# A weight conversion spread over six slots, and output products two tiles behind the gate in the first token block

## The chip, the cores and the metric

One core of one Trainium2 chip. TensorE multiplies matrices, VectorE and ScalarE work on elements, GpSimd does a few small operations, SyncE (SP) issues nearly all DMAs. The metric is device time in microseconds (us), the median of several executions.

## What is computed

Block attention, a gated feed-forward layer with RMS norm, and a second feed-forward layer with a rational activation, over 4608 tokens of width 512, all in float32:

```python
def _attn_ref(q, k, v):            # (8, 8, 576, 64), in chunks of 64 tokens
    scores = scale * np.matmul(q_c, k_c.transpose(0, 1, 2, 4, 3))
    scores = scores - np.max(scores, axis=-1, keepdims=True)
    attn = np.exp(scores)
    attn = attn / (np.sum(attn, axis=-1, keepdims=True) + 1e-09)
    return np.matmul(attn, v_c)

def _moe_ref(x, w_gate, w_val, w_out, rms_g):      # 512 -> 1536 -> 512
    rms = np.sqrt(np.mean(x * x, axis=-1, keepdims=True) + 1e-06)
    xn = x / rms * rms_g
    g = xn @ w_gate
    silu = g * (1.0 / (1.0 + np.exp(-g)))
    return silu * (xn @ w_val) @ w_out

def _moe2_ref(x, w_in, w_out, a, b):               # 512 -> 2048 -> 512
    h = x @ w_in
    P = a[0] + a[1] * h + a[2] * h**2 + a[3] * h**3
    Q = 1.0 + np.abs(b[0]) * np.abs(h) + np.abs(b[1]) * h**2
    return (P / (Q + 1e-06)) @ w_out
```

The weights of both layers reach the device as raw 64-bit words, two 32-bit words each, and the kernel turns each into a pair of rounded float32 numbers, a high and a low part.

## The kernel before

The tokens are cut into nine blocks j of 512, the 1536 features of the first layer into twelve tiles f of 128, those of the second into sixteen. Phase 1 runs over j and f, phase 2 over j and its sixteen tiles. Every matrix product is three passes (high x high, high x low, low x high) over four slices of depth: 12 matmuls of 128x512.

A **unit** u holds the three weight matrices of feature tile f=u: gate, val and output. It is converted once, in block 0, by six operations that `words_to_pair` lists after one DMA: L110 (ScalarE, first scaling), L114 (ScalarE, low word into `t`), L116 (VectorE, shift), L118 (VectorE, add), L121 (ScalarE, cast to the high part), L123 (VectorE, low part). Units 0 and 1 are converted in thirds, unit 2 and 3 as wholes; all of that and the first three feature tiles are interleaved by hand: each letter of `START` steps one generator (0 to 4 are attention tiles, a to f thirds of units 0 and 1, g, h, i are units 2, 3, 4, M, N, P the feature tiles 0, 1, 2, and each O is one output product). Units 4 to 11 are converted in the loop behind `START`.

That loop has three **slots** per feature tile: slot 3f holds the gate (12 matmuls, then tanh L386 on ScalarE and L388 on VectorE), slot 3f+1 val (12 matmuls, then L396 on VectorE, the cast L399 on ScalarE, L401 on VectorE, which give the pair r), slot 3f+2 one output product `p1_gemm2` (12 matmuls) of an earlier tile from the list `pend`. Ahead of a slot's own work `slot()` emits what the attention plan has there; behind it `weights(j, at)` emits the steps of units that `at_slots` put there, in the order in which they were entered, which is rising u. In block 0 the attention of block 1 has a tile each six slots: products (`xs`, with L250, L227, L229 on VectorE and L259, L236 on ScalarE) ahead of the gate of f=3, 5, 7, 9, a scale L356 two slots later, and transposes (`tp`, with L285, L292, L241 and the reciprocal on VectorE, L282 and L290 on ScalarE) ahead of val of f=4, 6, 8, 10.

The schedule is manual: each engine's instructions stand in the order in which the code emits them, and the waits are derived from the data and from the reuse of buffers. Buffers come from pools: 13 of "s3" (start tiles, raw words, converted units, later the stages of the second layer's weights), 3 of "s4" (the pairs r), 8 of "s2" (attention temporaries and u), 2 PSUM tiles "mm" for gate and val in turn, one "at" for attention, two "acc" for the output products.

Of the kernel before, what the change touches and what calls it, by code (L numbers as in the profile page):

```python
# [12 lines left out]
U32 = mybir.dt.uint32  # L13
# [6 lines left out]
P = 128  # L20
W = 512
CH = 64
U = 3
# [1 line left out]

START = (
    "0120d31230af041b0e0c1g002001012d21d02dd3011021d310320130123013230a3212a31321432aa13424a213a432bM"
    "3bb2b432e3bdcMbccecMMe4ecMMecgh4N4egMgNMgfNMgNONfghfPfhhNhfPNhfiOPhPPPP"
)

@with_exitstack
def fused_kernel(
# [36 lines left out]
    NSTART = 3  # L69
# [6 lines left out]
    def s3(name, shape=(P, U, 2, W), dtype=F32R):  # L76
        return sb.tile(list(shape), dtype, tag="s3", bufs=NS3, name=name)
# [22 lines left out]

    wt = {}

    def words_to_pair(high, low, t, hi, lo):

        nc.scalar.activation(  # L110
            out=high.bitcast(F32), in_=high.bitcast(F32), func=AF.Prelu, scale=2.0 ** -112, alpha=2.0 ** 32
        )
        yield
        nc.scalar.mul(t.bitcast(I32), low, 2.0 ** -29)  # L114
        yield
        nc.vector.tensor_scalar(out=high, in0=high, scalar1=3, scalar2=None, op0=ALU.logical_shift_left)  # L116
        yield
        nc.vector.tensor_tensor(out=high, in0=high, in1=t, op=ALU.add)  # L118
        yield
        x = high.bitcast(F32)  # L120
        nc.scalar.copy(hi, x)  # L121
        yield
        nc.vector.tensor_tensor(out=lo, in0=x, in1=hi.bitcast(F32), op=ALU.subtract)  # L123
        yield

    buffers = {}

    def unit(u, keys, part=None):

        if u not in buffers:  # L130
            buffers[u] = s3(f"raw{u}", (P, U, W, 2), U32), s3(f"w{u}", (P, 2, U, W))
        raw, whole = buffers[u]
        p = slice(0, U) if part is None else slice(part, part + 1)
        nc.sync.dma_start(
            out=raw[:, p].rearrange("p t f two -> p t (f two)"),
            in_=w1[u * U:u * U + U][p].rearrange("t p f -> p t f"),
        )
        yield
        for t, key in list(enumerate(keys))[p]:
            wt[key] = whole[:, :, t]  # L140
        if part is None:
            t = sb.tile([P, U, W], U32, tag="t", bufs=1, name=f"t{u}")
        else:
            t = att[(u * U + part) % TB].at[:, 5:6].bitcast(U32)
        yield from words_to_pair(raw[:, p, :, 1], raw[:, p, :, 0], t, whole[:, 0, p, :], whole[:, 1, p, :])

    w2d = [dram.tile([P, 2, U, W], F32, tag=f"w2d_{u}", name=f"w2d_{u}") for u in range(-(-2 * NF2 // U))]

    def stage(t):

        buf = s3(f"stage{t}")
        raw = buf[:, 0].rearrange("p two f -> p (two f)").bitcast(U32)
        pair = buf[:, 1]
        nc.sync.dma_start(out=raw, in_=w2[t])
        yield
        raw = raw.rearrange("p (f two) -> p f two", two=2)
        low = buf[:, 2, 0].bitcast(U32)
        yield from words_to_pair(raw[:, :, 1], raw[:, :, 0], low, pair[:, 0, :], pair[:, 1, :])
        nc.sync.dma_start(out=w2d[t // U][:, :, t % U], in_=pair.bitcast(F32))
        yield  # L160

    def unit2(u, keys):
        whole = s3(f"w2_{u}", (P, 2, U, W))
        n = len(keys)
        nc.sync.dma_start(out=whole[:, :, :n].bitcast(F32), in_=w2d[u][:, :, :n])
        for t, key in enumerate(keys):
            wt[key] = whole[:, :, t]
        yield
# [152 lines left out]
    def begin(i):  # L321

        start = i < TB
        yield from load(i, start)
        t = att[i]
        yield from products(None, t)
        yield from transposes(None, t)
        if start:
            yield from products(t, None)
            yield from transposes(t, None)  # L330

    def attention_plan(j):

        plan = {}
        if j + 1 == NB:
            return plan
        first = (j + 1) * TB

        starts = []
        gap, at, behind = (6, 9, 4) if j == 0 else (9, 1, 3)  # L340
        for n in range(TB):
            nxt = first + n + 1
            starts.append((at + n * gap, first + n, nxt if nxt < NB * TB else None))
        for at, x, s in starts:
            if s is not None:
                plan.setdefault(max(at - 3, 3 * NSTART if j == 0 else 0), []).append((loads, s))
            plan.setdefault(at, []).append((both, products, x, s))
            plan.setdefault(at + behind - 2, []).append((scale, x))
            plan.setdefault(at + behind, []).append((both, transposes, x, s))
        return plan  # L350
# [27 lines left out]
    pend = []  # L378
# [31 lines left out]
    def p1_products():  # L410
        while True:
            p1_gemm2()
            yield
# [43 lines left out]
    with tc.manual_schedule():  # L457

        def split(keys):
            return [keys[n:n + U] for n in range(0, len(keys), U)]  # L460

        first = split([(n, f) for f in range(NF1) for n in "gvo"])
        second = [unit2(u, keys) for u, keys in enumerate(split([(n, f) for f in range(NF2) for n in "iq"]))]
        work = {}

        def at_slots(x, slots, steps):
            for at, n in zip(slots, steps):
                work.setdefault(divmod(at, 3 * NF1), []).append((x, n))

        units = [None, None] + [unit(u, keys) for u, keys in enumerate(first)][2:]  # L470
        for u in range(4, NF1):
            slots = (3 * u - 10, 3 * u - 6, 3 * u - 5, 3 * u - 4, 3 * u - 3)
            at_slots(units[u], [max(at, 3 * NSTART) for at in slots][u == 4:], (1, 1, 2, 2, 1)[u == 4:])
        span = (NB - 2) * 3 * NF1
        for t in range(2 * NF2):
            at = 3 * NF1 + t * span // (2 * NF2)
            at_slots(stage(t), (at, at + 2, at + 3, at + 4, at + 5), (1, 2, 2, 2, 1))
        for u, x in enumerate(second):
            at_slots(x, ((NB - 1) * 3 * NF1 + 3 * u,), (1,))

        def weights(j, at):
            for x, n in work.pop((j, at), ()):
                for _ in range(n):
                    next(x)

        att.update((i, Tile(i, True)) for i in range(TB))
        gens = {str(i): begin(i) for i in range(TB + 1)}
        gens |= dict(zip("abcdef", (unit(u, first[u], t) for u in range(2) for t in range(U))))
        gens |= dict(zip("ghi", units[2:]))
        half = ((0, W // 2), (W // 2, W))  # L490
        gens |= dict(zip("MNP", (p1_cell(0, f, ((0, W),) if f else half) for f in range(NSTART))))
        gens["O"] = p1_products()
        next(gens["0"])
        nc.scalar.preload_act_table_set("exp_and_others")
        make_identity(nc, ident)
        nc.vector.memset(mhalf, -0.5)
        nc.vector.memset(lnb, (1.0 + 1e-6) * TWO_M63)
        nc.vector.memset(expb, -LN63)
        for step in START[START.index("0") + 1:]:
            next(gens[step])  # L500
            if step == "3" and "loaded" not in gens:
                gens["loaded"] = nc.sync.dma_start(out=gcol, in_=rms_g.rearrange("(k p) -> p k", p=P))
        nc.sync.dma_start(out=ab[:, 0:4], in_=pa.rearrange("(o n) -> o n", o=1).to_broadcast([P, 4]))
        nc.sync.dma_start(out=ab[:, 4:6], in_=pb.rearrange("(o n) -> o n", o=1).to_broadcast([P, 2]))
        nc.scalar.activation(out=absb1, in_=b1, func=AF.Abs)


        for j in range(NB):
            plan = attention_plan(j)
            at = 0 if j else 3 * NSTART  # L510

            def slot():
                for what, *of in plan.get(at, ()):
                    what(*of)

            def behind():
                nonlocal at
                weights(j, at)
                at += 1

            for f in range(0 if j else NSTART, NF1):
                if j == NB - 1 and f in (2, 3, 4, 5):
                    load_x2(0, f - 2)
                if j == NB - 1 and f in (3, 4, 5, 6):
                    split_x2(0, f - 3)
                slot()
                *_, u = p1_gate(j, f)
                behind()
                slot()
                run(p1_val(j, f, u))  # L530
                behind()
                slot()
                if len(pend) > 1:
                    p1_gemm2()
                behind()


    with tc.manual_schedule(engines={mybir.EngineType.Activation, mybir.EngineType.DVE}):
# [65 lines left out]
        for s in range(NS + 3):  # L604
            if s < NS:
                j, f = steps[s]
# [83 lines left out]
```

## Time and profile before

| | |
|---|---|
| median of 3 runs | 1794.75 us (1794.58 to 1794.98) |
| profiled execution | 1796.3 us |
| its span in the trace | 1794.5 us |
| mean granted TensorE clock | 0.996 of full speed |
| TensorE busy | 1761.6 us, 98% |

All times in a trace are counted from the span's start. "Busy" is the time in which an engine executes; matmuls are pipelined, so a busy TensorE isn't one at its peak. The page gives the whole span by engine, a table of stretches gives it by time, and the timeline gives single instructions.

### The profile page before, as it was taken

What the parts mean: (1) busy time and instruction counts of PE and PEld (TensorE: products, weight loads), DVE (VectorE), ACT (ScalarE), POOL (GpSimd) and SP (SyncE); (2) the same over time, 40 slices, a digit from 0 to 9 for tenths busy, and PEclk for the clock granted to TensorE, in tenths of its full rate; (3) what the DMA queues carried; (4) which work ended last, traced back from release to release, by engine and by line L of the source; (5) the groups of instructions that cost most, each with busy time, mean ns of one, the idle gap of its engine ahead of it and who ended that gap; (6) DMA issues with size and microseconds to landing.
All of it is one profiled execution on the core that took longest, in us unless ns stands there. A gap on an engine that the chain in (4) does not pass through costs nothing.

```text
span 1794.5 us, 24867 instructions
## 1 busy us (share of the span) xinstructions
PE 1761.6 (98%) x9960; PEld 1449.2 (81%) x9960; DVE 1144.9 (64%) x1693; ACT 913.7 (51%) x1485; POOL 261.8 (15%) x258
## 2 busy tenths in 40 slices
PE   6889999999999999999999999999999999999998
PEld 5668888888788888888888888888888888888887
DVE  8675444454444544544422688888888888888886
ACT  7563333332333333332221577777777677767775
POOL 0000000000000000000000132322233232323222
PEclk9999999999999999999999999999999999999999
DMA  9322213132222322212155201010101010101000
GB/s 355 138 89 83 94 54 107 53 107 83 100 72 83 104 68 95 88 65 94 43 193 189 88 13 41 7 41 7 41 7 41 7 48 1 48 0 48 0 24 24
DMA packets 51492, 127.44 MB, mean 71 GB/s; under 512 B 5680, under 2 KB 5680, under 8 KB 50096
## 3 DMA queue, kind: packets, MB, share of 16 engines
q1 hardware_dynamic: 51232, 125.59, 20.2%
q8 instruction: 78, 1.28, 0.3%
q14 instruction: 38, 0.31, 0.1%
q10 hardware_dynamic: 144, 0.26, 0.0%
HBM read 90.18 MB, written 35.65 MB: 70 GB/s over the span
## 4 chain that ended last, share of the span: by engine, by line
PE 91%; DVE 5%; issue 2%; ACT 1%; DMA 0%; POOL 0%; SPq 0%; DVEq 0%; ACTq 0%; POOLq 0%
PE o L585 22%; PE h L370 21%; PE vl L370 15%; PE a L427 15%; PE g L370 15%; PE xs L212 2%; DVE raw L118 1%; PE tp L275 1%; DVE w L123 1%; PE tp L278 1%; DVE raw L116 0%; DVE u L396 0%; DVE r L401 0%; DVE u L388 0%; DVE mx L227 0%
## 5 line engine op out<-in xcount | busy, mean ns | idle before, releaser
L585 PE MATMUL o<-w,gg 128*128 128x512 f32 x1728 | 416.4, 390 | 0.5 <-POOL gg L575 0.5
L370 PE MATMUL h<-x,w 128*128 128x512 f32 x1728 | 414.9, 389 | 0.0
L585 PEld LDWEIGHTS o<-w,gg 128*128 128x128 f32 x1728 | 323.6, 188 | 70.6 <-DVE ob L599 2.3
L370 PEld LDWEIGHTS h<-x,w 128*128 128x128 f32 x1728 | 324.3, 188 | 67.4
L370 PE MATMUL g<-xT,w 128*128 128x512 f32 (+1 forms) x1308 | 319.0, 393 | 11.5 <-DVE u L388 3.9
L370 PE MATMUL vl<-xT,w 128*128 128x512 f32 (+1 forms) x1308 | 320.2, 394 | 0.0
L427 PE MATMUL a<-r,w 128*128 128x512 f32 x1296 | 312.2, 389 | 1.8 <-DVE r L401 1.7
L370 PEld LDWEIGHTS g<-xT,w 128*128 128x128 f32 x1308 | 245.9, 190 | 66.1 <-DVE w L123 5.9
L427 PEld LDWEIGHTS a<-r,w 128*128 128x128 f32 x1296 | 243.1, 188 | 53.4 <-DVE r L401 2.5
L370 PEld LDWEIGHTS vl<-xT,w 128*128 128x128 f32 x1308 | 240.5, 189 | 49.3 <-DVE u L396 0.2
L575 POOL TENSOR_TENSOR gg<-T,gg 128x512 fp32r<-128x512 f32 x144 | 187.1, 1300 | 565.1 <-ACT gg L574 474.2
L388 DVE SCALAR_TENSOR_TENSOR u<-u,g 128x512 f32<-128x512 f32 x108 | 74.3, 688 | 302.5 <-ACT u L386 302.5
L386 ACT ACTIVATE u<-g 128x512 f32<-128x512 f32 x108 | 64.5, 597 | 290.3 <-PE g L370 290.2
L554 ACT ACTIVATE V<-h 128x512 f32<-128x512 f32 x144 | 86.0, 598 | 181.6 <-PE h L370 181.4
L399 ACT CAST r<-u 128x512 fp32r<-128x512 f32 x108 | 67.0, 621 | 214.0 <-DVE u L396 214.0
L557 DVE SCALAR_TENSOR_TENSOR V<-V,small,R 128x512 f32<-128x512 f32 x144 | 108.4, 753 | 78.3 <-ACT R L555 78.3
L261 POOL TENSOR_SCALAR ssq<-ssq 128x1 f32<-128x1 f32 x36 | 7.3, 203 | 852.1 <-ACT xf L259 833.8
L567 DVE SCALAR_TENSOR_TENSOR V<-V,R 128x512 f32<-128x512 f32 x144 | 99.9, 694 | 44.8 <-ACT R L566 44.8
L568 DVE SCALAR_TENSOR_TENSOR V<-V,R 128x512 f32<-128x512 f32 x144 | 124.1, 862 | 4.9
L401 DVE TENSOR_TENSOR r<-u,r 128x512 fp32r<-128x512 f32 x108 | 74.8, 693 | 73.4 <-ACT r L399 73.4
L396 DVE TENSOR_TENSOR u<-u,vl 128x512 f32<-128x512 f32 x108 | 72.6, 672 | 71.7 <-PE vl L370 71.7
L556 ACT ACTIVATE T<-h,small 128x512 f32<-128x512 f32 x144 | 112.6, 782 | 0.0
(107 smaller groups left out, 1535.0 us busy)
## 6 DMA issues: line engine op xcount, KB each, us to landing
stage<-in_w_dram SPq DMA_DIRECT2D x32, 512.0 KB, 3.7
w2d<-stage SPq DMA_DIRECT2D x32, 512.0 KB, 3.0
raw<-in_w_dram SPq DMA_DIRECT2D x10, 1536.0 KB, 8.8
w<-w2d SPq DMA_DIRECT2D x10, 1536.0 KB, 6.5
x2d<-x SPq DMA_DIRECT2D x36, 256.0 KB, 2.4
x2r<-x2d SPq DMA_DIRECT2D x36, 256.0 KB, 3.2
out_dram<-ob SPq DMA_DIRECT2D x36, 256.0 KB, 2.2
q<-in_qkv_dram SPq DMA_DIRECT2D x32, 256.0 KB, 3.7
```

The lines of the kernel that those rows point to most:

```text
L370: nc.tensor.matmul(out=acc[:, ts], lhsT=w[:, wh, wk], rhs=x[:, kk, xh, ts], start=kk == 0 and n == 0, stop=kk == KD - 1 and n == 2,)
L388: nc.vector.scalar_tensor_tensor(out=u, in0=u, scalar=1.0, in1=g, op0=ALU.add, op1=ALU.mult)
L396: nc.vector.tensor_tensor(out=u, in0=u, in1=vl, op=ALU.mult)
L401: nc.vector.tensor_tensor(out=r[:, 1, :], in0=u, in1=r[:, 0, :].bitcast(F32), op=ALU.subtract)
L427: nc.tensor.matmul(out=acc1[j][m], lhsT=wt["o", f][:, wh, ms], rhs=r[:, xh, :], start=f == 0 and n == 0, stop=f == NF1 - 1 and n == 2,)
L554: nc.scalar.activation(out=V, in_=h, func=AF.Square)
L556: nc.scalar.activation(out=T, in_=h, func=AF.Identity, scale=a3, bias=a2)
L557: nc.vector.scalar_tensor_tensor(out=V, in0=V, scalar=absb1, in1=R, op0=ALU.mult, op1=ALU.add)
L567: nc.vector.scalar_tensor_tensor(out=V, in0=V, scalar=1.0 + 1e-6, in1=R, op0=ALU.add, op1=ALU.mult)
L568: nc.vector.scalar_tensor_tensor(out=V, in0=V, scalar=-2.0, in1=R, op0=ALU.add, op1=ALU.mult)
L575: nc.gpsimd.tensor_tensor(out=r[:, 1, :], in0=T, in1=r[:, 0, :].bitcast(F32), op=ALU.subtract)
L585: nc.tensor.matmul(out=acc2[j][m], lhsT=r[:, rh, ms], rhs=wt["q", f][:, wh, :], start=f == 0 and n == 0, stop=f == NF2 - 1 and n == 2,)
```

## The change

- `unit` takes the buffer of the converted unit when the cast L121 is emitted and no longer together with the raw words' buffer at the load.
- The seven steps of a unit stand in six slots and not five: load, L110, L114 and L116, L118, L121, L123 in slots 3u-10, 3u-7, 3u-6, 3u-5, 3u-4, 3u-3. Before it was load, L110, L114 and L116, L118 and L121, L123 in 3u-10, 3u-6, 3u-5, 3u-4, 3u-3. None comes before slot 8 (before: 9), and the steps of slot 8 are emitted behind `START`, ahead of slot 9. Those are L110 to L121 of unit 4, the loads of units 5 and 6, and L110 of unit 5.
- `START` has one O less, and in block 0 the list `pend` is allowed two entries: tile f's slot has the output product of f-2. At j=1, f=0 two products run, and from there on it is one behind, as before.
- Attention loads stand one slot earlier.

```diff
-    "...MMecgh4N4egMgNMgfNMgNONfghfPfhhNhfPNhfiOPhPPPP"
+    "...MMecgh4N4egMgNMgfNMgNNfghfPfhhNhfPNhfiOPhPPPP"
...
-    def words_to_pair(high, low, t, hi, lo):
+    def words_to_pair(high, low, t, pair):
...
         x = high.bitcast(F32)
+        hi, lo = pair()
         nc.scalar.copy(hi, x)
...
-            buffers[u] = s3(f"raw{u}", (P, U, W, 2), U32), s3(f"w{u}", (P, 2, U, W))
-        raw, whole = buffers[u]
+            buffers[u] = [s3(f"raw{u}", (P, U, W, 2), U32), None]
+        raw = buffers[u][0]
...
+        def pair():
+            if buffers[u][1] is None:
+                buffers[u][1] = s3(f"w{u}", (P, 2, U, W))
+            whole = buffers[u][1]
+            for n, key in list(enumerate(keys))[p]:
+                wt[key] = whole[:, :, n]
+            return whole[:, 0, p, :], whole[:, 1, p, :]
...
-                plan.setdefault(max(at - 3, 3 * NSTART if j == 0 else 0), []).append((loads, s))
+                plan.setdefault(max(at - 4, 3 * NSTART if j == 0 else 0), []).append((loads, s))
...
         for u in range(4, NF1):
-            slots = (3 * u - 10, 3 * u - 6, 3 * u - 5, 3 * u - 4, 3 * u - 3)
-            at_slots(units[u], [max(at, 3 * NSTART) for at in slots][u == 4:], (1, 1, 2, 2, 1)[u == 4:])
+            slots = (3 * u - 10, 3 * u - 7, 3 * u - 6, 3 * u - 5, 3 * u - 4, 3 * u - 3)
+            at_slots(units[u], [max(at, 3 * NSTART - 1) for at in slots][u == 4:], (1, 1, 2, 1, 1, 1)[u == 4:])
...
+            if j == 0:
+                weights(0, at - 1)
...
-                if len(pend) > 1:
+                while len(pend) > (1 if j else 2):
                     p1_gemm2()
```

## Rows read from the trace of the kernel before

**Rows 1.** The page, first part: each engine's busy us (share of span) and instructions.
```profile
PE 1761.6 (98%) x9960; PEld 1449.2 (81%) x9960; DVE 1144.9 (64%) x1693; ACT 913.7 (51%) x1485; POOL 261.8 (15%) x258
```
**Rows 2.** Stretches: us, busy time (instructions) by engine, PEclk, DMA share, GB/s.
```profile
60.00:140.00 80.00, 69.10 (x466) 53.73 (x465) 58.95 (x71) 48.08 (x51) 2.22 (x6) 0.94 0.27 99
140.00:220.00 80.00, 80.00 (x541) 65.96 (x540) 40.40 (x67) 26.44 (x47) 2.23 (x6) 1.00 0.24 80
```
**Rows 3.** Timeline, tile f=6: start, us, engine line operation [idle before <-releaser].
```profile
91.93 1.75 DVE L118 CUSTOM_DVE_ANT_0 raw<-raw,t 128x3072 uint16<-128x3072 uint16 x1
93.71 1.58 ACT L121 CAST w<-raw 128x1536 fp32r<-128x1536 f32 x1 [2.15 <-DVE raw L118]
95.20 0.60 ACT L386 ACTIVATE u<-g 128x512 f32<-128x512 f32 x1
...
95.69 1.63 ACT L110 ACTIVATE raw<-raw 128x1536 f32<-128x1536 f32 x1
95.83 0.69 DVE L388 SCALAR_TENSOR_TENSOR u<-u,g 128x512 f32<-128x512 f32 x1 [2.15 <-ACT u L386]
96.44 1.75 DVE L123 TENSOR_TENSOR w<-raw,w 128x1536 fp32r<-128x1536 f32 x1
...
103.06 0.95 DVE L116 TENSOR_SCALAR raw<-raw 128x1536 uint32<-128x1536 uint32 x1
104.14 1.76 DVE L118 CUSTOM_DVE_ANT_0 raw<-raw,t 128x3072 uint16<-128x3072 uint16 x1
```
**Rows 4.** Timeline, tile f=7: the scale and the next L118.
```profile
114.30 0.48 DVE L356 TENSOR_SCALAR xa<-xa,ssq 128x512 f32<-128x512 f32 x1
114.70 1.75 DVE L118 CUSTOM_DVE_ANT_0 raw<-raw,t 128x3072 uint16<-128x3072 uint16 x1
```
**Rows 5.** Timeline from the end of the start order to tile f=3.
```profile
40.33 1.75 DVE L123 TENSOR_TENSOR w<-raw,w 128x1536 fp32r<-128x1536 f32 x1
...
46.67 3.18 PE L427 MATMUL a<-r,w 128*128 128x512 f32 x11 [1.07 <-DVE r L401]
...
49.68 2.88 PE L370 MATMUL vl<-xT,w 128*128 128x512 f32 x12
...
53.85 0.20 ACT L505 ACTIVATE small<-small 128x1 f32<-128x1 f32 x1
...
57.70 1.61 ACT L110 ACTIVATE raw<-raw 128x1536 f32<-128x1536 f32 x1
...
59.21 1.61 ACT L114 ACTIVATE t<-raw 128x1536 int32<-128x1536 uint32 x1
...
60.85 1.76 DVE L118 CUSTOM_DVE_ANT_0 raw<-raw,t 128x3072 uint16<-128x3072 uint16 x1 [0.55 <-ACT t L114]
...
69.17 1.75 DVE L118 CUSTOM_DVE_ANT_0 raw<-raw,t 128x3072 uint16<-128x3072 uint16 x1
```
**Rows 6.** Timeline, tiles f=9 and 10: the last L118, transposes, val.
```profile
137.46 1.75 DVE L118 CUSTOM_DVE_ANT_0 raw<-raw,t 128x3072 uint16<-128x3072 uint16 x1
...
138.79 0.60 PE L278 MATMUL tp<-ident,xa 128*128 128x128 f32 x4
139.14 2.98 PE L370 MATMUL vl<-xT,w 128*128 128x512 f32 x12
```
**Rows 7.** The chain that ended last, one output product in it: start, us, what.
```profile
142.13 2.72 PE a L427 x12
```
**Rows 8.** SP's timeline: the raw loads of units 5, 6 and 7.
```profile
34.82 7.65 SPq L134 DMA_DIRECT2D raw<-in_w_dram  x3
```
**Rows 9.** The page, DMA issues: count, KB each, median us from issue to landing.
```profile
raw<-in_w_dram SPq DMA_DIRECT2D x10, 1536.0 KB, 8.8
```
**Rows 10.** Timeline, the last ten gate matmuls of f=6 and f=10.
```profile
88.82 2.57 PE L370 MATMUL g<-xT,w 128*128 128x512 f32 x10 [0.94 <-DVE w L123]
...
134.35 4.06 PE L370 MATMUL g<-xT,w 128*128 128x512 f32 x10 [0.94 <-DVE w L123]
```
**Rows 11.** A stretch in the second of these gates, columns as in rows 2.
```profile
136.00:138.00 2.00, 2.00 (x6) 1.53 (x5) 2.00 (x4) 1.11 (x1) 0.00 (x0) 0.50 0.24 49
```

More of the change, by code (lines that the diff above doesn't have):

```diff
@@ L27 @@
     "0120d31230af041b0e0c1g002001012d21d02dd3011021d310320130123013230a3212a31321432aa13424a213a432bM"
-    "3bb2b432e3bdcMbccecMMe4ecMMecgh4N4egMgNMgfNMgNONfghfPfhhNhfPNhfiOPhPPPP"
+    "3bb2b432e3bdcMbccecMMe4ecMMecgh4N4egMgNMgfNMgNNfghfPfhhNhfPNhfiOPhPPPP"
 )
@@ L138, in unit @@
         yield
-        for t, key in list(enumerate(keys))[p]:
-            wt[key] = whole[:, :, t]
         if part is None:
@@ L144, in unit @@
             t = att[(u * U + part) % TB].at[:, 5:6].bitcast(U32)
-        yield from words_to_pair(raw[:, p, :, 1], raw[:, p, :, 0], t, whole[:, 0, p, :], whole[:, 1, p, :])
+        def pair():
[5 more added lines that the diff above has]
+            return whole[:, 0, p, :], whole[:, 1, p, :]
+        yield from words_to_pair(raw[:, p, :, 1], raw[:, p, :, 0], t, pair)
     w2d = [dram.tile([P, 2, U, W], F32, tag=f"w2d_{u}", name=f"w2d_{u}") for u in range(-(-2 * NF2 // U))]
@@ L157, in stage @@
         low = buf[:, 2, 0].bitcast(U32)
-        yield from words_to_pair(raw[:, :, 1], raw[:, :, 0], low, pair[:, 0, :], pair[:, 1, :])
+        yield from words_to_pair(raw[:, :, 1], raw[:, :, 0], low, lambda: (pair[:, 0, :], pair[:, 1, :]))
         nc.sync.dma_start(out=w2d[t // U][:, :, t % U], in_=pair.bitcast(F32))
```

## The prediction

> **What bounds the kernel now.** I read the page's first part first. TensorE is busy 98% of the span [rows 1], so the most that a change of order can bring is the idle part, and the next question is where that lies. The table by stretches answers it: from 60 to 140 us TensorE is busy 69.10 of 80 us at a mean granted clock of 0.94; from 140 to 220 us it is busy 80.00 of 80 [rows 2]. So the change acts where there is something to win, in block 0 while the weights are still being converted, and nowhere else: after about 139 us TensorE runs without a gap, and whatever time block 0 takes is handed on to the end unchanged.
>
> Who holds TensorE there? The timeline of one feature tile f=6 and the next [rows 3, 4]. The reader is to follow the order on VectorE and ScalarE: VectorE adds the words of unit 7 (L118, 91.93), ScalarE's rounding cast (L121, 93.71) waits for it, the tanh of the gate (L386, 95.20) stands behind that cast in ScalarE's queue, and VectorE, which has nothing else in front of it, waits 2.15 us for the tanh before L388 (95.83). Then come L123, the attention steps, the product u and the low part r, the shift L116 and the next L118 (104.14). That is a closed ring, L118 to L118: 12.21 us in a tile with transposes (91.93 to 104.14) and 10.56 us in one with attention products (104.14 to 114.70), 22.77 us for two tiles. VectorE is busy only 58.95 of the 80 us [rows 2]: it isn't full, it is waiting in a ring with ScalarE. Each member is there because of a datum or because its engine takes its queue in the order in which the code emits it, and the rows show both [rows 3] (the tanh has its input long before and still starts after the cast). TensorE is not a member: the gate of tile f+1 waits for its result.
>
> **The change, part by part.** I name the steps of unit u by their lines: L110 (first scaling, ScalarE), L114 (low word, ScalarE), L116 (shift, VectorE), L118 (add, VectorE), L121 (cast, ScalarE), L123 (low part, VectorE).
>
> *The six slots.* Old order: L110 behind the tanh and L123 of the tile; L114 and L116 behind val; L118 and L121 behind the output product. New: L110 one slot earlier, which is the slot of L121 of the unit before. The list of a slot is filled by rising u, so ScalarE gets L121(u), then L110(u+1), then the tanh. L114 and L116 follow the tanh and L123; L118 follows r. No instruction is added and none removed; what changes is which lie in the ring.
> - L110 enters the ring, between cast and tanh. Back to back on ScalarE it takes 1.51 us (57.70 to 59.21) [rows 5]. Today it runs after the tanh, under VectorE's L388 and L123 [rows 3], and costs nothing. The cover is gone: VectorE has at that point only the scale L356 (0.40) or the three attention steps, which already fit into today's wait. Behind it are queued the square, exp and tanh; for the tanh wait L388 and everything after it on VectorE.
> - L116 moves from before L118 to after L123: same engine, same ring. Today L118 starts 1.08 us after L116 (103.06 to 104.14) though L116 lasts 0.95, the rest being L114; with L114 earlier it is 0.88. Gain 0.20 in tiles with transposes.
> - In tiles with products L356 (114.30 to 114.70, 0.40) comes to stand behind L118, in VectorE's wait. Gain 0.40 there [rows 4].
>
> So the ring becomes 12.21 + 1.51 - 0.20 = 13.52 and 10.56 + 1.51 - 0.40 = 11.67 us, 25.19 for two tiles instead of 22.77.
>
> *Unit 4 before slot 9.* Today its whole conversion is emitted after the gate of f=3, with L110 at 57.70 [rows 5]. Now it comes right behind the start order, so L110(4) follows the small Abs (53.85, 0.20) at once, and the f=3 tile is already a ring of the new kind.
>
> *Output products one further behind.* o(1) leaves the start order and o(f-2) runs at f; at j=1, f=0 two run. 12 matmuls of 2.72 us [rows 7] each time, as many in all. The start gains: today g(2) (42.49), o(1) and then val(2), because o(1) had to wait for r(1) and for its weights until 46.67 and ends near 49.7 [rows 5]. Now after val(1) comes g(2), held by L123(2) to 40.33 + 1.75 = 42.08; its last 10 matmuls (2.72 / 12 us each) end near 44.4, o(0) (nothing to wait for) at 47.1, and val(2) starts there instead of at 49.68: 2.55 us earlier. From val(2) to the end of the Abs is 54.05 - 49.68 = 4.37 us, so L110(4) starts at 47.13 + 4.37 = 51.5, L114 1.51 later, L118(4) 1.64 later (59.21 to 60.85), at 54.65; the ring of f=3 takes 11.67, and L118(5) starts at 66.3 instead of 69.17 [rows 5]: 2.85 us won.
>
> *Then the ring.* From L118(5) to L118(11) there are six tiles, f=4 to 9, three of each kind, each with the L110 of another unit (6 to 11) in it: 3 x 25.19 = 75.57, so L118(11) starts at 141.9, today at 137.46 [rows 6]: 4.4 us lost. After L118(11) now comes L356 (1.76 + 0.48), at which the transposes of f=10 wait: the half with xa starts at 144.1, val(10) at 144.5, against 139.14 [rows 6]: 5.4 us late (today L356 comes ahead of L118 [rows 4]). From val(10) on TensorE has no gap in either: g(11) needs L123(11), which ends near 148, and TensorE comes to it at 144.5 + 2 x 2.72 = 149.9. But at val(10) only o(0) to o(7) are done, one product fewer than before: 2.72 us of TensorE's work still stands behind. Sum: 5.4 + 2.7 = **8.1 us slower**.
>
> *Late result buffers.* A buffer is taken at the cast and not at the load. On the chip that is no instruction. It could make L121 wait for a buffer: the nearest one to come free is the raw of unit u-1, last read by L123(u-1), which stands ahead of L118(u) on VectorE, so nothing at the low end; and nothing to gain, since L121 waits for L118 anyway [rows 3]. The loads may start earlier. Three of the raw loads of units 5 to 7 are issued by 42.5 us and used from 57.70 on or later [rows 8, 5], so earlier brings nothing. The other side: SP's queue now has units 5 and 6 ahead of tile 5's q, k and v, and tile 6's ahead of unit 7. Tile 5 is needed at 50 us, some 15 us after its neighbours in the queue were issued; unit 7 at 80. I take 0, with 3 us (a load that is late by a third of its 8.8 us to landing [rows 9]) as the upper end.
>
> *Earlier attention loads* (a slot): q, k and v are used a whole ring later. 0.
>
> **TensorE's clock.** Row first: the last ten matmuls of g(6) and of g(10) both came after a wait of 0.94 us; g(6)'s took 2.57 us, at a granted clock of 1.00, and g(10)'s 4.06 us, going down to 0.50, the 1.2 GHz level [rows 10, 11]. Low stretches within the ring cost nothing, as TensorE waits there anyway. The Trainium skill says (TensorE: Matmul & The Clock Gate, HAM oscillation — how this bites in real kernels) that a matmul burst behind each long wait begins at the half clock. The trace agrees in part: not behind every wait. As a mechanism here it concerns only val(10), the first burst of the stretch without gaps, and is the second rival below.
>
> **The rivals.**
> - *The ring as worked out*: +8.1 us. For: every term but one is a difference of starts in one ring. Against: the start gain rests on g(2) at full clock. Own range +5.5 to +10.5. Chance 0.64.
> - *The clock is low behind the last wait.* TensorE's waits grow (six groups of 2.72 us, 16.3 us, and the attention's matmuls in 25.2 us instead of 22.8), so val(10) may start at 1.2 GHz. By these two gates [rows 10] a burst of ten then costs 4.06 - 2.57 = 1.5 us more, so +9.6 for one such burst and +11 for two. The skill's rule named above would give the first of these. Chance 0.13.
> - *A load comes late* (units 5 and 6 ahead of q, k, v): +8.1 and up to 3 more, 1806. Chance 0.05.
> - *The six slots don't put L110 between cast and tanh* (the change doesn't do what it says, or ScalarE runs L110 while it waits for L118): then each ring loses its 0.20 or 0.40 and f=3 gains 1.5 more: -2.85 - 1.5 - 1.8 at L118(11), + 1.0 at val(10) for L356, + 2.7 for the product: -2.4, 1792.3, no difference that can be told. Against: ScalarE stands idle for 2.15 us before the cast and takes nothing from behind it [rows 3]. Chance 0.09.
> - *Faster*: one mechanism, at the gate of f=4 and each second one after it: the tanh ceases to wait for the cast, because the conversion gets ahead of the matmuls; the ring opens and TensorE is the bound. That decides if L118 starts before val's matmuls of its tile end. Then the 10.9 us of idle between 60 and 140 us [rows 2] go: 1784. Against: VectorE lags today by most of a tile, and the ring's edges don't depend on TensorE. Chance 0.09.
>
> **How the numbers follow.** The profiled execution took 1796.3 us with a span of 1794.5; the plain runs have the median 1794.75. All terms are differences within the span, so they are added to the median: 1794.75 + 8.1 = 1802.9. The range takes in the first three cases (0.82): 1799 by the low end of the forecast's own, widened to 1798 for a start gain of 4 us, and 1807.5 for clock and load. A measurement of this kernel can tell about 0.2% (3.6 us) from no change: faster 0.09, same 0.10 (the fourth case and the forecast's lowest edge), slower 0.81.
>
> **What would show it.** In the changed trace: val(2) near 47 instead of 49.68; L118 of unit 5 near 66; on ScalarE the order L121, L110, tanh, and a wait of VectorE before L388 of 3 to 3.7 us instead of 2.15 in tiles with transposes; two tiles in 25.2 us; TensorE's busy share from 60 to 145 us lower than today; val(10) near 144.5; no difference after it but the two products at j=1. It is wrong if L110 is found behind the tanh, if the two-tile period stays at 22.8 or falls, or if the output products fill waits that I took to be closed to them.

## The result

The changed kernel takes 1804.03 us in the median of four executions (1803.88 to 1807.42), the kernel before 1794.77 in the same comparison: ratio 1.0056, 95% interval 1.0039 to 1.0073; the medians differ by 9.3 us. Executions of the kernel before fall into two groups, near 1794.6 and near 1796.4 us in the later comparisons, so that a median moves by a few tenths with their mix. The profiled execution of the changed kernel is the 1807.42 one, with a span of 1805.6 us; the three plain ones lie at 1803.88 to 1804.09. Against the profiled execution of before the span is 11.1 us longer, and the places below add up to that.

The diff adds lines, so in the changed kernel the cast is L122 (was L121), the low part L124 (L123), the scale L364 (L356), the tanh L394 (L386), the step behind it L396 (L388), u L404 (L396), the transposes L283 and L286 (L275 and L278), gate and val L378 (L370), output products L435 (L427). L110, L116 and L118 keep their numbers.

First the table of stretches of the changed kernel (us, then busy time of TensorE, its weight loads, VectorE, ScalarE, GpSimd, each with its instructions, then granted clock, DMA share, GB/s), to be held beside [rows 2]:

```profile
60.00:150.00 90.00, 74.79 (x470) 57.89 (x469) 60.02 (x74) 48.32 (x55) 2.97 (x8) 0.89 0.30 105
150.00:220.00 70.00, 70.00 (x435) 57.78 (x433) 31.36 (x54) 20.67 (x36) 1.49 (x4) 1.00 0.24 80
```

TensorE stands for 15.2 us of this stretch, where it stood for 10.9 in the kernel before, at a clock of 0.89 instead of 0.94. From 150 to 220 us it runs without a gap, as it did from 140 to 220. So the loss is made in block 0, and it is kept.

Who holds TensorE there shows in the timeline of tile f=6, the one of [rows 3]:

```profile
93.22 1.75 DVE L118 CUSTOM_DVE_ANT_0 raw<-raw,t 128x3072 uint16<-128x3072 uint16 x1
...
94.89 0.48 DVE L364 TENSOR_SCALAR xa<-xa,ssq 128x512 f32<-128x512 f32 x1
95.01 1.60 ACT L122 CAST w<-raw 128x1536 fp32r<-128x1536 f32 x1 [2.43 <-DVE raw L118]
...
96.51 1.58 ACT L110 ACTIVATE raw<-raw 128x1536 f32<-128x1536 f32 x1
98.00 0.58 ACT L394 ACTIVATE u<-g 128x512 f32<-128x512 f32 x1
...
98.60 0.69 DVE L396 SCALAR_TENSOR_TENSOR u<-u,g 128x512 f32<-128x512 f32 x1 [3.23 <-ACT u L394]
...
106.70 1.75 DVE L118 CUSTOM_DVE_ANT_0 raw<-raw,t 128x3072 uint16<-128x3072 uint16 x1
```

The reader sees L110 between the cast and the tanh, 1.49 us from its start to that of the tanh. VectorE waits 3.23 us for the tanh, where it waited 2.15, and L118 to L118 takes 13.48 us, where it took 12.21. The list of VectorE's waits gives the sum of the tiles in a stretch (engine, line, for whom: us in total, times, longest); this is the line of the changed kernel from 60 to 150 us, with tiles f=3 to 10 in it:

```profile
DVE u L396 <- ACT u L394: 22.8, 8, 3.3
```

The same wait in the kernel before, from 60 to 140 us, with tiles f=4 to 9:

```profile
DVE u L388 <- ACT u L386: 10.5, 6, 2.2
```

In the changed kernel these six tiles alone have 18.2 us.

The end of the ring in the changed kernel, the lines that answer to [rows 6] (g(f), val(f) and o(f) are the gate, the val and the output product of tile f; the last line has the two products at j=1):

```profile
143.41 1.75 DVE L118 CUSTOM_DVE_ANT_0 raw<-raw,t 128x3072 uint16<-128x3072 uint16 x1
...
145.61 1.08 PE L286 MATMUL tp<-ident,xa 128*128 128x128 f32 x4 [1.92 <-DVE xa L364]
146.34 4.27 PE L378 MATMUL vl<-xT,w 128*128 128x512 f32 x12
...
150.45 2.88 PE L435 MATMUL a<-r,w 128*128 128x512 f32 x12
...
168.09 5.60 PE L435 MATMUL a<-r,w 128*128 128x512 f32 x24
```

val(10) starts at 146.34 and not at 139.14: 7.2 us. It stands behind a wait of 1.92 us for the scale, which now comes after L118, and it runs at a low clock (0.61 from 146 to 150 us): 4.11 us until the next product instead of some 2.8, that is 1.3 more. One product more stands behind it, 2.72 us. 7.2 + 1.3 + 2.7 = 11.2, the 11.1 us of the two spans.

And the start, which answers to [rows 5]:

```profile
40.51 0.73 PE L378 MATMUL g<-xT,w 128*128 128x512 f32 x2 [1.31 <-ACT w L122]
...
42.35 3.86 PE L378 MATMUL g<-xT,w 128*128 128x512 f32 x10 [1.12 <-DVE w L124]
...
46.01 3.26 PE L435 MATMUL a<-r,w 128*128 128x512 f32 x12
...
49.11 2.88 PE L378 MATMUL vl<-xT,w 128*128 128x512 f32 x12
```

g(2) follows val(1) at once, waits for its weights until 42.3, and then took 3.86 us for ten matmuls that take 2.57 at full clock (the granted clock was 0.82 from 42 to 44 us and 0.50 from 44 to 46); val(2) starts at 49.11, before at 49.68. Most of the start's gain is gone in this execution.

### The profile page after: what moved, and what is told of

It reads as the page before. It is cut to its first block, busy times and chain, and to the rows that moved or that the text cites. A ratio compares the mean times of both kernels' runs of the same rounds, so it can differ in the third digit from the quotient of the medians.

```text
span 1805.6 us, 24860 instructions
## 1 busy us (share of the span) xinstructions
PE 1769.7 (98%) x9960; PEld 1456.4 (81%) x9960; DVE 1144.8 (63%) x1693; ACT 913.3 (51%) x1485; POOL 262.0 (15%) x258
## 4 chain that ended last, share of the span: by engine, by line
PE 91%; DVE 3%; issue 2%; ACT 2%; DMA 1%; POOL 0%; SPq 0%; ACTq 0%; POOLq 0%; DVEq 0%
PE o L595 22%; PE h L378 21%; PE vl L378 15%; PE a L435 15%; PE g L378 15%; PE xs L220 2%; PE tp L283 1%; PE tp L286 1%; DVE raw L118 1%; ACT raw L110 1%; DVE w L124 0%; DVE raw L116 0%; DVE u L396 0%; DMA raw<-in_w_dram 0%; DVE u L404 0%
## 5 line engine op out<-in xcount | busy, mean ns | idle before, releaser
L378 PE MATMUL h<-x,w 128*128 128x512 f32 x1728 | 414.9, 389 | 0.0
L378 PEld LDWEIGHTS h<-x,w 128*128 128x128 f32 x1728 | 324.4, 188 | 67.4
L378 PE MATMUL g<-xT,w 128*128 128x512 f32 (+1 forms) x1308 | 323.8, 397 | 13.6 <-DVE u L396 8.0
L378 PE MATMUL vl<-xT,w 128*128 128x512 f32 (+1 forms) x1308 | 321.5, 395 | 0.0
L435 PE MATMUL a<-r,w 128*128 128x512 f32 x1296 | 311.5, 389 | 0.0
L378 PEld LDWEIGHTS g<-xT,w 128*128 128x128 f32 x1308 | 249.1, 193 | 69.3 <-DVE u L396 9.7
L435 PEld LDWEIGHTS a<-r,w 128*128 128x128 f32 x1296 | 243.7, 188 | 50.7
L378 PEld LDWEIGHTS vl<-xT,w 128*128 128x128 f32 x1308 | 241.7, 190 | 49.5
L396 DVE SCALAR_TENSOR_TENSOR u<-u,g 128x512 f32<-128x512 f32 x108 | 74.3, 688 | 314.9 <-ACT u L394 314.9
L394 ACT ACTIVATE u<-g 128x512 f32<-128x512 f32 x108 | 64.4, 597 | 294.1 <-PE g L378 294.0
L404 DVE TENSOR_TENSOR u<-u,vl 128x512 f32<-128x512 f32 x108 | 72.5, 672 | 69.6 <-PE vl L378 69.6
```

Source lines behind the costliest of these rows:

```text
L378: nc.tensor.matmul(out=acc[:, ts], lhsT=w[:, wh, wk], rhs=x[:, kk, xh, ts], start=kk == 0 and n == 0, stop=kk == KD - 1 and n == 2,)
L396: nc.vector.scalar_tensor_tensor(out=u, in0=u, scalar=1.0, in1=g, op0=ALU.add, op1=ALU.mult)
L404: nc.vector.tensor_tensor(out=u, in0=u, in1=vl, op=ALU.mult)
L435: nc.tensor.matmul(out=acc1[j][m], lhsT=wt["o", f][:, wh, ms], rhs=r[:, xh, :], start=f == 0 and n == 0, stop=f == NF1 - 1 and n == 2,)
```

## The experiments

The theory (**ring**): L110 between cast and tanh lengthens a ring of VectorE and ScalarE that sets the pace of block 0. The rivals: the second product behind (**two behind**), the late **buffers**, the **clock**. "Six tiles" are f=4 to 9, from L118 of unit 5 to L118 of unit 11: 68.29 us in the kernel before, 75.29 in the changed one.

**L110 alone, put into the kernel before.**

```diff
-            slots = (3 * u - 10, 3 * u - 6, 3 * u - 5, 3 * u - 4, 3 * u - 3)
+            slots = (3 * u - 10, 3 * u - 6 - (u > 5), 3 * u - 5, 3 * u - 4, 3 * u - 3)
```

> The kernel before with one edit: L110 of units 6 to 11 is emitted a slot earlier, which puts it behind the cast of the unit before and ahead of the tanh. Nothing else is moved. Ring theory: each of the six tiles f=4 to 9 takes 1.51 us longer (13.7 and 12.1 us), L118(11) starts near 146.5 instead of 137.46, 1802.5 to 1805. If the loss of the changed kernel comes from its other parts: 1794 to 1797.

Measured: 1804.02 us, ratio 1.005 (1.0036 to 1.0063). Its timeline at f=6:

```profile
94.75 1.78 DVE L118 CUSTOM_DVE_ANT_0 raw<-raw,t 128x3072 uint16<-128x3072 uint16 x1
...
96.56 1.60 ACT L121 CAST w<-raw 128x1536 fp32r<-128x1536 f32 x1 [2.13 <-DVE raw L118]
...
98.06 1.59 ACT L110 ACTIVATE raw<-raw 128x1536 f32<-128x1536 f32 x1
...
99.56 0.58 ACT L386 ACTIVATE u<-g 128x512 f32<-128x512 f32 x1
...
100.16 0.69 DVE L388 SCALAR_TENSOR_TENSOR u<-u,g 128x512 f32<-128x512 f32 x1 [3.63 <-ACT u L386]
```

VectorE's wait grew from 2.15 to 3.63 us, the next L118 starts at 108.48, a ring of 13.73. L118(5) stands at 69.10 as in the kernel before, L118(11) at 146.15: six tiles in 77.05 us, 8.76 more. One instruction of 1.5 us that moves by a slot, in six tiles, is enough for a loss of this size.

**L110 ahead of the cast, in the changed kernel.** The reverse: same slot, other order.

```diff
-        def at_slots(x, slots, steps):
-            for at, n in zip(slots, steps):
-                work.setdefault(divmod(at, 3 * NF1), []).append((x, n))
+        def at_slots(x, slots, steps, early=None):
+            for i, (at, n) in enumerate(zip(slots, steps)):
+                held = work.setdefault(divmod(at, 3 * NF1), [])
+                held.insert(0 if i == early else len(held), (x, n))
...
-            at_slots(units[u], [max(at, 3 * NSTART - 1) for at in slots][u == 4:], (1, 1, 2, 1, 1, 1)[u == 4:])
+            at_slots(units[u], [max(at, 3 * NSTART - 1) for at in slots][u == 4:], (1, 1, 2, 1, 1, 1)[u == 4:], 1 if u > 5 else None)
```

> The kernel after, except that in a shared slot the first scaling L110 of units 6 to 11 is emitted ahead of the cast L121 of the unit before it, instead of behind it. If the lengthened ring is the cause (L110 between cast and tanh), L110 now runs in ScalarE's wait before the cast, the two-tile ring falls from 25.1 us to about 22.2 us (12.0 and 10.2), L118(11) starts 7 to 9 us earlier than in the kernel after, and the time comes to 1793.5 to 1796. If the second output product behind, or the late buffers, or the clock is the cause, it stays at 1802 to 1804.

Measured: 1796.86 us (1795.20 to 1797.37), ratio 1.0004 (0.9995 to 1.0014). The timeline at f=6:

```profile
88.27 1.66 ACT L110 ACTIVATE raw<-raw 128x1536 f32<-128x1536 f32 x1
...
89.00 1.75 DVE L118 CUSTOM_DVE_ANT_0 raw<-raw,t 128x3072 uint16<-128x3072 uint16 x1
...
90.79 1.60 ACT L122 CAST w<-raw 128x1536 fp32r<-128x1536 f32 x1 [0.86 <-DVE raw L118]
...
92.29 0.59 ACT L394 ACTIVATE u<-g 128x512 f32<-128x512 f32 x1
...
101.01 1.75 DVE L118 CUSTOM_DVE_ANT_0 raw<-raw,t 128x3072 uint16<-128x3072 uint16 x1
```

L110 now fills ScalarE's wait for L118 (0.86 us of it are left, of 2.43), the tanh follows the cast, and the ring is 12.01 us. Six tiles take 66.49 us, L118(5) 66.86 to L118(11) 133.35, 8.8 less than in the changed kernel. The time is 7.2 us lower than that of the changed kernel, 0.9 above what was expected. What the ring gives is not all handed on: val(10) starts 2.62 us behind L118(11), as the scale stands behind it, and one product is left over.

**The slots without two behind.** The changed kernel with the second O back and `if len(pend) > 1`.

> The kernel after with the output products one tile behind again (the second O of the start order put back, one entry allowed in the list). By the ring theory the start gain of 2.5 us and the 2.7 us of products left over both go, and the ring stays: 1801.5 to 1803.5. If the second product behind were the cause of the loss, this would come back to 1794 to 1796.

Measured: 1803.31 us, ratio 1.0042 (1.0027 to 1.0057). L118(5) at 68.64, L118(11) at 143.95: six tiles in 75.31 us, the changed kernel's. Two behind isn't the cause.

**Two behind without the slots.** The kernel before with one O less and `while len(pend) > (1 if j else 2)`.

> The kernel before with nothing but the output products of block 0 two tiles behind (one O less, two entries allowed). Ring theory: val(2) starts 0.6 to 2.5 us earlier, the ring is as before, 2.7 us of products are left over at its end: 1794.7 to 1796.7. If two behind were the cause: 1801 to 1804. If the products fill the waits before the gates, as one could intend: under 1793.

Measured: 1796.76 us (1794.81 to 1796.94), ratio 1.0004 (0.9994 to 1.0014). In its profiled execution g(2)'s ten matmuls again took long (3.90 us), val(2) came at 48.86; the six tiles took 68.25 us as before, and val(10)

```profile
137.15 3.00 PE L370 MATMUL vl<-xT,w 128*128 128x512 f32 x12
```

came 2.0 us earlier than in [rows 6], against a product of 2.72 us left over. Of the 2.0 us only 0.87 are L118(11)'s, 136.59 and not 137.46; the rest is g(10), whose last ten matmuls took 2.57 us here and 4.06 in [rows 10]. It doesn't last: val(11) waits 0.88 us for u (L396), for TensorE now reaches it before VectorE has caught up, and starts at 146.47 where it started at 147.40. So 0.93 us are won up to val(11), and 2.72 are owed behind it. That the span, 1794.8 us, is all the same only 0.3 us longer than before's comes of a burst far behind block 0, shown in the last section.

**Unit 4 early alone.** The kernel before with L110 to L121 of unit 4 ahead of slot 9.

> The kernel before with nothing but the four first conversion steps of unit 4 (L110 to L121) emitted ahead of slot 9. Ring theory: L118(5) starts 1 to 1.5 us earlier than 69.17, the rest of the ring is unchanged and carries the gain to the end: 1793.2 to 1794. If the stretch from 53 to 66 us is held by something else (a load, TensorE): 1794.7.

Measured: 1793.57 us (1793.15 to 1794.90), ratio 0.9992 (0.9983 to 1.0001): no difference that is clear, by the interval. The trace has the step as expected:

```profile
67.69 1.75 DVE L118 CUSTOM_DVE_ANT_0 raw<-raw,t 128x3072 uint16<-128x3072 uint16 x1
...
135.93 1.75 DVE L118 CUSTOM_DVE_ANT_0 raw<-raw,t 128x3072 uint16<-128x3072 uint16 x1
```

1.5 us earlier at the beginning of the six tiles and at their end.

**The late buffers alone**, in the kernel before.

> The kernel before with nothing but the late result buffers (the converted unit's buffer taken at the cast). It frees loads only, which were early enough: 1794.5 to 1795.2, the seven L118 of units 5 to 11 at the same times as before within 0.3 us. If the buffers cause part of the loss (a cast that waits for one), above 1797.

Measured: 1794.87 us, ratio 1.0003 (0.9993 to 1.0012). L118(5) at 69.13, L118(11) at 137.40: 0.04 and 0.06 us from before. Nothing, on either side.

**Both corrected: L110 ahead of the cast, one behind.**

> The kernel after with both corrected: L110 of units 6 to 11 ahead of the cast of the unit before, and the output products one tile behind. Ring theory: L118(5) at 68.6 us as with one behind, six tiles of 12.0 and 10.2 us, L118(11) at 135.1, val(10) at 137.7 instead of 139.14, nothing left over: 1793.0 to 1794.2. If the gain of two behind at the start were kept by something else, or if the spread slots cost anything beside L110's place, it stays at 1795 or above.

Measured: 1795.00 us (1792.86 to 1796.75), ratio 0.9998 (0.9989 to 1.0007). The ring did as expected, L118(5) 68.81 and L118(11) 135.27, but the time didn't come down with it. Its end:

```profile
137.47 0.66 PE L286 MATMUL tp<-ident,xa 128*128 128x128 f32 x4 [1.90 <-DVE xa L364]
137.88 4.58 PE L378 MATMUL vl<-xT,w 128*128 128x512 f32 x12
```

val(10) starts at 137.88, 1.3 us earlier than before, and takes 4.58 us: TensorE had stood for the scale behind L118, and the clock of 138 to 142 us was 0.59. So the new place of the scale costs too: by the wait, and in this execution by the clock behind it.

**The scale ahead of L118.** The last kernel, with the scale emitted behind r and ahead of L118 in block 0, and unit 5's L110 in slot 9 (behind the tanh of f=3) and not in slot 8.

```diff
-            plan.setdefault(at + behind - 2, []).append((scale, x))
+            plan.setdefault(("late", at + 1) if j == 0 else at + behind - 2, []).append((scale, x))
...
+            if u == 5:
+                slots = (8, 9, 9, 10, 11, 12)
...
             def behind():
                 nonlocal at
+                for what, *of in plan.get(("late", at), ()):
+                    what(*of)
                 weights(j, at)
```

> The changed slots with the three orders corrected: L110 ahead of the cast of the unit before (unit 5's behind the tanh of f=3), the scale L356 ahead of L118, output products one behind. Ring theory: f=3 as in the kernel with unit 4 early (L118(5) at 67.7 us), tiles of 12.0 and 10.55 us, L118(11) at 135.4, no wait of the transposes for the scale, val(10) at 136.9 to 137.5: 1792.3 to 1793.5, ratio to the kernel before 0.9985 to 0.9993. If the transposes or the clock take it back: 1794.5 or above.

Measured: 1792.27 us (1792.03 to 1794.02), ratio 0.9986 (0.9977 to 0.9995), faster than both kernels.

```profile
134.93 1.75 DVE L118 CUSTOM_DVE_ANT_0 raw<-raw,t 128x3072 uint16<-128x3072 uint16 x1
...
135.07 0.66 PE L286 MATMUL tp<-ident,xa 128*128 128x128 f32 x4 [0.23 <-DVE xa L364]
135.48 3.01 PE L378 MATMUL vl<-xT,w 128*128 128x512 f32 x12
```

The scale is back in the ring (six tiles take 67.56 us, 1.1 more), but val(10) starts 0.55 us after L118(11) and not 2.61, and at full clock. The whole gain isn't the scale's. L118(5) stands at 67.37 and not at 68.81; 1.06 of these 1.44 us lie in the ring of f=3, which unit 5's L110 has left. And val(11) waits 0.92 us for u: it starts at 144.85, 9.92 us behind L118(11). An estimate from that distance: with L118(11) 1.44 us later val(11) would start near 146.3, against 147.79 in the last kernel, where val(10) lost 1.57 us to the clock. So by this estimate the scale's new place alone gives little but the escape from that low burst; no run has it alone. In the experiment with L110 first, too, the transposes of f=10 waited 1.88 us for the scale, and a product was left over; that this is all of its missing gain isn't shown, as val(10) ran at full clock in its profiled execution.

**The cast behind the tanh.** Could the edge from L118 over the cast to the tanh be cut? One behind, unit 4 early; units 5 to 11 with

```diff
-            slots = (3 * u - 10, 3 * u - 7, 3 * u - 6, 3 * u - 5, 3 * u - 4, 3 * u - 3)
+            slots = (3 * u - 10, 3 * u - 6, 3 * u - 5, 3 * u - 4, 3 * u - 3, 3 * u - 2)
...
```

> One behind, late buffers and unit 4 early as in the kernel after, but units 5 to 11 in the slots 3u-10, 3u-6, 3u-5, 3u-4, 3u-3, 3u-2: the cast L121 behind the tanh of its slot and L123 behind the low part of r, so that the tanh no longer stands behind a cast that waits for VectorE. By the ring theory the edge L118 to cast to tanh to L388 is cut: two tiles take about 20.7 us instead of 22.8 (bound by VectorE's own work and the waits for r, exp and tanh), val(10) comes 5 to 6 us earlier: 1787.5 to 1791. If the gate then waits for L123 as long as it waited for the tanh, the time stays at 1793 to 1796; if L123 so late holds each gate, it is above 1797.

Measured: 1807.42 us, ratio 1.0071 (1.0054 to 1.0088): my forecast of a gain failed, the last branch came. TensorE's gate of f=5 in it:

```profile
79.69 4.63 PE L378 MATMUL g<-xT,w 128*128 128x512 f32 x10 [4.06 <-DVE w L124]
```

L123 (here L124) comes so late that the gate waits for it, and val and the tanh stand behind the gate: the ring now runs through TensorE, 25.1 us for two tiles (80.65 to 105.79). This burst ran at the low clock, 4.63 us for ten matmuls, so here the clock is part of the ring. In tiles with transposes the ring goes on from the tanh over the cast and L110 to the copy pT (L290), for which VectorE waits 2.71 us at f=6.

**One tile further ahead.** To take TensorE out of that ring again, units 6 to 11 were converted a tile earlier.

```diff
+            slots = (3 * u - 10, 3 * u - 9, 3 * u - 8, 3 * u - 7, 3 * u - 6, 3 * u - 5)
...
+            if u == 5:
+                slots = (8, 9, 9, 9, 9, 10)
```

> One behind, late buffers and unit 4 early as in the kernel after, but units 6 to 11 converted one feature tile further ahead: L110 3u-9, L114 and L116 3u-8, L118 3u-7, L121 behind the tanh of 3u-6, L123 behind r of 3u-5 (unit 5 catches up in slots 9 and 10). The tanh then stands behind no cast that waits for VectorE, and no gate waits for an L123 of its own tile. By the ring theory the tiles f=3 and 4 lose some 2 to 3 us for the extra unit, the two-tile period falls to 20 to 21 us, val(10) starts near 133.5: 1788.5 to 1791.5. If VectorE's and ScalarE's ring isn't the bound but TensorE's own waits for weights, or loads, it stays at 1793 to 1797.

Measured: 1803.43 us, ratio 1.0049 (1.0032 to 1.0065): wrong again. No gate of f=5 to 10 waits for weights, and still L118 to L118 over two tiles is 25.0 us (87.67 to 112.68). VectorE's waits, 60 to 150 us:

```profile
DVE r L409 <- ACT r L407: 9.8, 7, 3.1
DVE xf L293 <- ACT pT L290: 9.2, 4, 3.1
DVE u L396 <- ACT u L394: 6.1, 5, 1.3
```

The wait for the tanh shrank to 6.1 us, and two others took its place: the cast of r and the copy pT stand behind the cast of the unit and L110, which had been moved ahead of them. In tiles with transposes the cast still starts only after L118 (3.33 to 3.39 us of wait), L110 and pT follow it, and VectorE waits for pT. The 3 us of ScalarE were pushed from one of VectorE's waits into the next.

## Why the prediction was right

**The ring.** Predicted 13.52 and 11.67 us for the two kinds of tile and 75.57 for six. Measured 13.48 to 13.50 and 11.58 to 11.64, 75.29 in all. L110's price of 1.51 us, taken from two neighbouring starts of ScalarE [rows 5], is 1.49 in the changed kernel's timeline, and the experiment that moves it alone gave 8.76 us for six tiles, against 6 x 1.51 = 9.06. The two credits, 0.20 for L116 and 0.40 for the scale, are in the difference of the two: 75.29 against 77.05 is 1.76 for six tiles, foretold 1.80, and it lies where it was foretold: 0.16 to 0.25 in tiles with transposes, 0.35 to 0.44 in the others.

**The start.** Predicted: val(2) at 47.1, L118(5) at 66.3, a gain of 2.85 us. In the profiled execution 49.11 and 68.12, a gain of 1.05. The term that failed is g(2) "at full clock": its ten matmuls took 3.86 us and not 2.57, and o(0) 3.1 until val(2) and not 2.72. In the experiment with L110 first g(2) took 2.56 us, val(2) came at 47.83 and L118(5) at 66.86: there the step is as foretold but for some 0.6 us, by which g(2)'s ten matmuls began later (42.71 and not 42.08).

**The end.** The wait for the scale, the product left over and TensorE without gaps from val(10) on were all found; val(10) at 146.34 instead of 144.5 carries the start's 1.8 us. The sentence that TensorE has no gap after about 139 us was read from rows up to 220 only: at 478 us it waits 1.69 us for a load of k, in the changed kernel 1.71 at 490. As both kernels have this wait, the loss is handed on all the same. That val(10) ran at the low clock was the second rival. In the profiled execution it happened, and at g(2) as well, +11.1 in the span, above the +10.5 that the first case allowed itself. The three plain executions lie 9.2 us above the median of before, with a granted clock of 0.993 to 0.994 against 0.990 in the profiled one; which of their bursts were low no trace shows. The median, 9.3 us, would fit the forecast's 8.1 us and one low burst, at g(2) or at val(10); that isn't shown.

**Terms taken at nothing.** Late buffers: 0.4 us by the medians, within the interval, and L118's starts unchanged. Loads: SP issued units 5 and 6 at 31.4 us and tile 5's q, k, v at 33.8 to 34.8, ahead of any use; no cast and no L110 waited for a load, and no wait of TensorE from 40 to 150 us ends with one. The earlier attention loads weren't run alone; the kernel with the scale ahead has them and is faster than before. The rival of a late load fell.

**Rivals that fell.** "The slots don't put L110 there" falls by the timeline. "Faster, as the ring opens" falls too, and the last two experiments say why: when the tanh no longer waits for the cast, TensorE's gate or ScalarE's copies close the ring anew. In the prediction I took the tanh to be the only place where ScalarE's conversion work could hold VectorE.

**Where my later expectations were wrong.** With L110 first I priced only the ring, 1793.5 to 1796, and left out the wait of the transposes for the scale, 1.88 us at f=10, and the clock that a wait can cost; it came to 1796.9. In its profiled execution val(10) ran at full clock, so how much the clock took in the others stays open. The two attempts to cut the ring were off by some 18 and 13 us, both by counting VectorE's queue alone and not who waits behind the moved steps; in the first the low clock of the gates in the ring was left out, too.

## What to carry to other kernels

Where two engines hand work to and fro, find the ring, and price an edit by what enters or leaves it: an instruction of 1.5 us that cost nothing on one side of a wait cost its whole length, six times, on the other, in the same slot. Before a step is moved "to where the engine is idle", look at what ends that idle time, and put the step ahead of the instruction that waits, not behind it. And what is won at the start by deferring work is owed where the bound engine runs without gaps again.

## What the runs showed of the hardware

The clock behind a wait isn't a fixed price. In the changed kernel each second gate from f=6 on stood 0.94 us for its low part, after a wait of 1.9 us, and its ten matmuls then took 4.14 us at f=6, 4.63 at f=8 and 2.55 at f=10. The burst that counted was val(10): 4.27 us in the changed kernel and 4.58 in the one with both corrected, behind a wait of 1.9 us for the scale, 3.01 behind the same wait (1.88) in the kernel with L110 first, 3.01 behind one of 0.23. The Trainium skill's rule that a burst behind a long wait begins at the half clock (TensorE: Matmul & The Clock Gate, HAM oscillation — how this bites in real kernels) is told there of longer waits, some 3 to 5 us for a load. Behind these shorter ones it held for f=6 and 8 and not for f=10; here the measurement decides.

The same place shows both outcomes far from any change, too. These are the kernel before and the one with two behind alone, at a wait for a load of k that TensorE has in every kernel here, long behind block 0:

```profile
478.42 0.69 PE L212 MATMUL xs<-k,q 64*64 64x64 f32 x32 [1.69 <-DMA k<-in_qkv_dram]
479.05 4.61 PE L370 MATMUL vl<-xT,w 128*128 128x512 f32 x12
```
```profile
480.32 0.69 PE L212 MATMUL xs<-k,q 64*64 64x64 f32 x32 [1.74 <-DMA k<-in_qkv_dram]
480.95 3.02 PE L370 MATMUL vl<-xT,w 128*128 128x512 f32 x12
```

The granted clock was 0.59 from 480 to 484 us in the first and 1.00 in the second. Behind this wait of 1.52 to 1.85 us the burst took 4.25 to 4.62 us in nine of the twelve profiled executions and 3.01 to 3.06 in three. It goes into the span: from val(11) to the end the kernel before takes 1647.1 us, the one with two behind, its product left over taken off, 1645.6. Whoever compares two profiled executions looks at such a burst first. A shorter wait ahead of the stretch without gaps may save more than the wait, but no run here shows that by itself.
